# A gated SSM and dense kernel on one core: first tokens turned in 128-row pieces by plain matmuls, first weights on the ScalarE queue, small parameters on the GpSimd queue, B in two parts, third GELU stage ahead of the first outputs

## Chip, cores, metric

The kernel runs on one core of one Trainium2 chip. The metric is the device time of one execution in microseconds (us), as the median of several executions.

Times "at 4.47" are microseconds from the start of the profiled execution's span. The span leaves out about 1.5 to 2 us of the device time, so spans and medians are not mixed in one subtraction.

Names: PE is TensorE, PEld its weight load, DVE is VectorE, ACT is ScalarE, POOL is GpSimd, SP is SyncE. "ACTq" and "SPq" are their instruction streams when they issue DMAs.

## The reference

For 2048 tokens of width 640, the result is `g * a + (1 - g) * b`, where

```python
g = sigmoid((x * gate_w).sum(-1, keepdims=True))
# a: diagonal complex state-space layer (640 states)
dt = exp(log_dt); Lam_bar = exp(dt * Lam)
Bu = einsum("bld,pd->blp", x, ((Lam_bar - 1) / Lam)[:, None] * Bmat)
h[t] = Lam_bar * h[t-1] + Bu[t]
a = 2 * real(einsum("blp,dp->bld", h, Cmat)) + x * Dskip
# b: dense layer, 640 -> 1728 -> 640
b = gelu(x @ w1 + b1) @ w2 + b2
```

Inputs and output are bfloat16.

## The kernel before

The tokens go through in four chunks of 512 (`CH`). For each chunk TensorE does four kinds of stage: the projection by B ("ssm", 50 matmuls of 512 columns), the first dense layer ("FF1"), the second ("FF2", `fin_b`), and the outputs by C (`fin_a`). Chunk 0's FF1 is the first stage, behind a few matmuls without use (the warm-up). For it, half of chunk 0 is transposed on TensorE, from tokens loaded as they lie in memory (`xn`). The other half comes transposed by a DMA. The weights of FF1 are loaded in two blocks: `w1a` (first 6 of 14 column blocks, 192 KB for each of five row blocks) and `w1b`. `prmA` holds three short parameter vectors, 15 rows of 128 numbers; turned into columns on TensorE they feed all of the tables that the scan needs.

The loads, in program order, and the first work:

```python
    load_xn(0, 0, H)                                                    # 320 KB, SP
    nc.scalar.dma_start(out=prmA[0:KS, :], in_=A_log_dt...)             # three small loads, ACT
    nc.scalar.dma_start(out=prmA[KS:2 * KS, :], in_=A_Lambda_im...)
    nc.scalar.dma_start(out=prmA[2 * KS:3 * KS, :], in_=A_Lambda_re...)
    for kd in range(KD):                                                # five times 192 KB, SP
        nc.sync.dma_start(out=w1a[kd][:], in_=B_w1[kd * P:(kd + 1) * P, 0:cut1])
    nc.sync.dma_start_transpose(out=xT[0][:, :, H * P:CH], in_=x2d[H * P:CH, :])
    for kd in range(KD):
        nc.sync.dma_start(out=w1b[kd][:, 0:F - cut1], in_=B_w1[kd * P:(kd + 1) * P, cut1:F])
    make_identity(nc, ident[:])
    # ... (iota and memsets on POOL; prmB on ACT; b1x on SP)
    nc.sync.dma_start_transpose(out=BT_re[:], in_=A_B_re[:, :])
    nc.sync.dma_start_transpose(out=BT_im[:], in_=A_B_im[:, :])
    # ... (further loads)
    for _ in range(6):                                                  # warm-up
        nc.tensor.matmul(wps[:], lhsT=warm[:, 0:P], rhs=warm[:], start=True, stop=True)
    # ...
    for kd in range(KD):
        for a in range(H):
            nc.tensor.transpose(pT[kd][:, a * P:(a + 1) * P], xn[0][:, a, kd * P:(kd + 1) * P], ident[:])
    nc.tensor.transpose(pA[:, 0:3 * KS], prmA[:], ident[0:3 * KS, 0:3 * KS])
    # ... (copies to xT on DVE and ACT; table work)
    for kd in range(KD):                                                # 30 matmuls of 256 columns
        for kf in range(FA):
            ff1_mm(banks[kf], 0, kf, kd, 0, HT)
    # ...
    for kd in range(KD):                                                # 30 more, on the DMA-transposed half
        for kf in range(FA):
            ff1_mm(banks[kf], 0, kf, kd, HT, CH)
```

The order of the stages, as the end of the kernel's text lists them: ssm(0), FF1(1), ssm(1), FF2(0), outputs(0), ssm(2), FF1(2), FF2(1), outputs(1), and so on.

Of the kernel before, what the change touches and what calls it, by code (L numbers as in the profile page):

```python
# [10 lines left out]
ALU = mybir.AluOpType  # L11
ACT = mybir.ActivationFunctionType
BF16 = mybir.dt.bfloat16
F32 = mybir.dt.float32
I32 = mybir.dt.int32
# [12 lines left out]
TPC = CH // P  # L28
HD = D // 2
# [9 lines left out]
def kernel(  # L39
# [32 lines left out]
    def bank(dtype=F32):  # L72
        return ps.tile([P, CH * 4 // (4 if dtype == F32 else 2)], dtype, name="bank")
# [8 lines left out]
    BT_re = const.tile([P, KD, D], BF16, name="BT_re")  # L82
    BT_im = const.tile([P, KD, D], BF16, name="BT_im")
# [5 lines left out]
    prmA = const.tile([3 * KS, P], BF16, name="prmA")  # L89
    NB = KS + KF - 1  # L90
    prmB = const.tile([NB, P], BF16, name="prmB")
# [9 lines left out]
    warm = work.tile([P, CH], BF16, name="v")  # L101
# [8 lines left out]

    H = TPC // 2

    def load_xn(c, a0=0, a1=TPC):
        if a0 == 0:
            xn[c] = xnp.tile([P, TPC, D], BF16, name="xn")
        r0 = c * CH + a0 * P
        nc.sync.dma_start(out=xn[c][:, a0:a1, :], in_=x2d[r0:r0 + (a1 - a0) * P, :].rearrange("(a p) d -> p a d", p=P))

    load_xn(0, 0, H)
    nc.scalar.dma_start(out=prmA[0:KS, :], in_=A_log_dt.rearrange("(j p) -> j p", p=P))  # L120
    nc.scalar.dma_start(out=prmA[KS:2 * KS, :], in_=A_Lambda_im.rearrange("(j p) -> j p", p=P))
    nc.scalar.dma_start(out=prmA[2 * KS:3 * KS, :], in_=A_Lambda_re.rearrange("(j p) -> j p", p=P))
    for kd in range(KD):
        nc.sync.dma_start(out=w1a[kd][:], in_=B_w1[kd * P:(kd + 1) * P, 0:cut1])  # L124
    nc.sync.dma_start_transpose(out=xT[0][:, :, H * P:CH], in_=x2d[H * P:CH, :])  # L125
    for kd in range(KD):
        nc.sync.dma_start(out=w1b[kd][:, 0:F - cut1], in_=B_w1[kd * P:(kd + 1) * P, cut1:F])  # L127
    make_identity(nc, ident[:])
    HC = CH // 4
    tfi = work.tile([P, HC], I32, name="e")  # L130
    nc.gpsimd.iota(tfi[:], pattern=[[1, HC]], base=0, channel_multiplier=0)
    nc.gpsimd.memset(b1x[:, F_LAST:F_LAST + 1], 0.0)
# [3 lines left out]
    nc.scalar.dma_start(out=prmB[KS:NB, :], in_=B_b1[0:(KF - 1) * P].rearrange("(j p) -> j p", p=P))  # L136
    nc.scalar.dma_start(out=prmB[0:KS, :], in_=gate_w.rearrange("(j p) -> j p", p=P))
    nc.sync.dma_start(out=b1x[:, 0:F_LAST], in_=B_b1[F - F_LAST:F].rearrange("(o d) -> o d", o=1).to_broadcast([P, F_LAST]))  # L138
    nc.sync.dma_start_transpose(out=BT_re[:], in_=A_B_re[:, :])  # L139
    nc.sync.dma_start_transpose(out=BT_im[:], in_=A_B_im[:, :])  # L140
# [15 lines left out]
    class Clock:  # L156
        pe = 5.0
        act = 13.0
# [5 lines left out]
    def later(ready, cost, fn):  # L164
        pend.append((ready, cost, fn))

    def let_out(until):
        while pend:
            ready, cost, fn = pend[0]
            start = max(ck.dve, ready)  # L170
            if start >= until:
                return
            pend.pop(0)
            fn()
            ck.dve = start + cost
# [14 lines left out]
    nc.vector.memset(warm[:], 0.0)  # L190
# [3 lines left out]
    wps = bank()  # L194
    for _ in range(6):
        nc.tensor.matmul(wps[:], lhsT=warm[:, 0:P], rhs=warm[:], start=True, stop=True)
    nc.tensor.matmul(wps[:, 0:2 * P], lhsT=warm[:, 0:P], rhs=warm[:, 0:2 * P], start=True, stop=True)
    pA = bank(BF16)
    pT = [bank(BF16) for _ in range(KD)]
    for kd in range(KD):  # L200
        for a in range(H):
            nc.tensor.transpose(pT[kd][:, a * P:(a + 1) * P], xn[0][:, a, kd * P:(kd + 1) * P], ident[:])
    HT = H * P
    nc.tensor.transpose(pA[:, 0:3 * KS], prmA[:], ident[0:3 * KS, 0:3 * KS])

    def col(name, dtype=F32, n=KS):
        return const.tile([P, n], dtype, name=name)
# [7 lines left out]
    for kd in range(KD):  # L215
        dst = xT[0][:, kd, 0:HT]
        if kd % 2 == 0:
            nc.vector.tensor_copy(out=dst, in_=pT[kd][:, 0:HT])
        else:
            nc.scalar.activation(out=dst, in_=pT[kd][:, 0:HT], func=ACT.Identity)  # L220
    nc.vector.tensor_copy(out=colA[:], in_=pA[:, 0:3 * KS])
    nc.scalar.activation(out=dt16[:], in_=ldt_c, func=ACT.Exp)
    nc.vector.tensor_copy(out=dt32[:], in_=dt16[:])
    nc.vector.tensor_tensor(out=dtl[:], in0=dt32[:], in1=lre_c, op=ALU.mult)
    nc.vector.tensor_tensor(out=th_c[:], in0=dt32[:], in1=lim_c, op=ALU.mult)
    nc.vector.tensor_scalar(out=thp_c[:], in0=th_c[:], scalar1=INV_2PI, scalar2=None, op0=ALU.mult)
    nc.scalar.activation(out=r_c[:], in_=dtl[:], func=ACT.Exp)


    scr = gelp.tile([P, KF * CH // 2], F32, name="gel")  # L230
    HB = 2 * HC

    def scratch(i):
        return scr[:, i * KS * HC:(i + 1) * KS * HC].rearrange("p (k i) -> p k i", k=KS)

    u, red, ab = scratch(0), scratch(1), scratch(2)
    m1, m2 = scratch(3), scratch(4)
    FSC = hsp.tile([P, 2 * KS, HB], F32, name="hs")
    FS = FSC[:, 0:KS, :]
    FC = FSC[:, KS:2 * KS, :]  # L240
    NQ = 4
    two = col("two", n=NQ * KS)
    kq = col("kq", I32, n=NQ * KS)
    redq = col("redq", n=NQ * KS)
    absq = col("absq", n=NQ * KS)
    sq = col("sq", n=NQ * KS)
    cq = col("cq", n=NQ * KS)
    kk = work.tile([P, KS, HC], I32, name="bu", bufs=8)

    def over(c):  # L250
        return c.rearrange("p (k o) -> p k o", o=1).to_broadcast([P, KS, HC])

    nc.vector.tensor_tensor(out=u, in0=tf[:].rearrange("p (o i) -> p o i", o=1).to_broadcast([P, KS, HC]), in1=over(thp_c[:]), op=ALU.mult)
    nc.vector.tensor_copy(out=kk[:], in_=u)
    nc.vector.tensor_tensor(out=red, in0=u, in1=kk[:], op=ALU.subtract)
    sth, cth = sq[:, 0:KS], cq[:, 0:KS]
    sL, cL = sq[:, KS:2 * KS], cq[:, KS:2 * KS]
    sH, cH = sq[:, 2 * KS:3 * KS], cq[:, 2 * KS:3 * KS]
    sQ, cQ = sq[:, 3 * KS:4 * KS], cq[:, 3 * KS:4 * KS]


# [3 lines left out]
    def ff1_mm(p, c, kf, kd, t0=0, t1=CH):  # L265
        w = w1a[kd][:, kf * P:(kf + 1) * P] if kf < FA else w1b[kd][:, (kf - FA) * P:(kf - FA + 1) * P]
        nc.tensor.matmul(p[:, t0:t1], lhsT=w, rhs=xT[c][:, kd, t0:t1], start=(kd == 0), stop=(kd == KD - 1))  # L267
        pe(t1 - t0)
# [33 lines left out]
    def ff1(c, k0=0):  # L302
        for kf in range(k0, KF - 1):
            p = bank()
            if kf == KF - 3:
                last = last_bank(c)
            for kd in range(KD):
                ff1_mm(p, c, kf, kd)
            ff1_act(p, c, kf)
            let_out(ck.pe)  # L310
        last_tile(c, *last)
        let_out(ck.pe)

    def gel_tile(c):
        gel[c] = gelp.tile([P, KF, CH], BF16, name="gel")


    gel_tile(0)
    banks = [bank() for _ in range(FA)]
    for kd in range(KD):  # L320
        for kf in range(FA):
            ff1_mm(banks[kf], 0, kf, kd, 0, HT)
# [10 lines left out]
    for kd in range(KD):  # L333
        for kf in range(FA):
            ff1_mm(banks[kf], 0, kf, kd, HT, CH)
        if kd == 2:
            nc.tensor.transpose(pA[:, P:P + NB], prmB[:], ident[0:NB, 0:NB])
            nc.vector.tensor_copy(out=colB[:], in_=pA[:, P:P + NB])
            for j in range(KD):
                nc.vector.tensor_copy(out=w1b[j][:, n1b - 1:n1b], in_=pA[:, P + j:P + j + 1])  # L340
# [69 lines left out]
    def scan_ops(c, ks, bu, ready):  # L410
# [58 lines left out]
        later(0, 0.7, f8)  # L469

    def ssm(c):
        hs[c] = hsp.tile([P, 2 * KS, CH], BF16, name="hs")
        for ks in range(KS):
            bu = work.tile([P, 2, CH], BF16, name="bu", bufs=8)
            for ri, BT in enumerate((BT_re, BT_im)):
                p = bank()
                for kd in range(KD):
                    nc.tensor.matmul(p[:], lhsT=BT[:, kd, ks * P:(ks + 1) * P], rhs=xT[c][:, kd, :],  # L478
                                     start=(kd == 0), stop=(kd == KD - 1))
                    pe(CH)  # L480
                nc.scalar.activation(out=bu[:, ri, :], in_=p[:], func=ACT.Identity)  # L481
                act(0.6)
            scan_ops(c, ks, bu, ck.act)
            if c == 0 and ks == 0:
                later(0, 1.6, factors)
            let_out(ck.pe)
# [27 lines left out]
    def fin_b(c):  # L514
        for a in range(TPC):
# [3 lines left out]
            if a >= TPC - 2:  # L519
                seed(c * TPC + a - (TPC - 2))  # L520
# [12 lines left out]
    def fin_a(c):  # L533
        for a in range(TPC):
# [33 lines left out]
    fin_b(0)  # L568
    fin_a(0)
    load_xn(2)  # L570
    ssm(2)
    gel_tile(2)
    ff1(2)
    fin_b(1)
    gates(2)
# [41 lines left out]
```

## Time and profile before

| | before |
|---|---|
| median of 3 runs (range) | 217.63 us (217.43 to 217.79) |
| span of the profiled execution | 216.2 us |
| PE busy | 211.9 us, 98% |
| first FF1 matmul | 5.26 |
| first projection matmul | 21.13 |
| gapless from, to | 22.49, 213.17 |

The page's first part gives the busy time of each engine, and its second part rows of 40 slices, here the granted TensorE clock in tenths:

```profile
PE 211.9 (98%) x1368; PEld 128.2 (59%) x1368; DVE 189.8 (88%) x393; ACT 91.7 (42%) x156; POOL 1.6 (1%) x12
...
PEclk9999999999999999999999999999999999999999
```

The clock row takes what lies before the first clock change in the trace as full, and that change is the rise at 6.95.

TensorE is the bound. The chain of waits of the kernel before, followed back from the last instruction, shows from where it has been so (columns: start, duration, what; "SPq" is SP issuing a DMA):

```profile
0.73 3.17 DMA xn<-in_A_x_dram
...
4.77 2.04 SPq L125
...
9.85 5.63 SPq L139
...
15.52 6.92 DMA BT_im<-in_A_B_im_dram
...
22.49 9.89 PE bank L478 x45
32.38 14.03 PE bank L267 x65
```

The chain goes through loads until 22.49 and through TensorE alone after that, to 213.17. The timeline of PE in the kernel before shows the first part (columns: start, time, engine, line, operation, names, shapes, count, and in brackets the idle time before and what ended it):

```profile
1.18 2.74 PE L196 MATMUL bank<-v 128*128 128x512 bf16 x6 [1.18 <-DVE halfpi L191]
...
3.95 1.26 PE L202 MATMUL bank<-ident,xn 128*128 128x128 bf16 x10
5.14 0.19 PE L204 MATMUL bank<-ident,prmA 15*128 15x15 bf16 x1
5.26 6.22 PE L267 MATMUL bank<-xT,w1a 128*128 128x256 bf16 x48
...
12.84 5.56 PE L267 MATMUL bank<-xT,w1b 128*128 128x512 bf16 x25
...
21.13 1.24 PE L478 MATMUL bank<-xT,BT_re 128*128 128x512 bf16 x5
22.49 1.25 PE L478 MATMUL bank<-xT,BT_im 128*128 128x512 bf16 x5
```

FF1 starts at 5.26 and goes on with hardly a gap to 21.13; then five projection matmuls, a wait for the imaginary part of B, and no gap any more. If those five matmuls were put in front of 22.49 without the wait, the gapless run would begin at 21.41 (22.49 less 5 x 0.216). The view of one tile gives the time from issue to landing of its loads; this is the line for `w1a`:

```profile
DMA to landing us min/median/max: 3.1/3.5/3.8
```

It covers the landings that the view could assign, here those of the first two of five blocks. The trace keeps every update of the loads' semaphores (counters by which the program waits), and from them the five land at 4.38, 5.59, 6.09, 6.82 and 7.71, at most 3.9 us after their issue.

The view of SP's waits has this line (columns: total us, times, longest):

```profile
SPq L124 <- DMA xn<-in_A_x_dram: 1.3, 1, 1.3
```

The fourth `w1a` (L124) waits until the tokens have landed: 2.65 to 3.92. It is the program that waits. In the trace the loads of SP and ACT take eight semaphores in turn (numbers 100, 102, 103 and 105 to 109), so the ninth load is held until the load that had its semaphore before has landed.

### The profile page before, as it was taken

To read this page: it belongs to the slowest core of one execution; us is meant where nothing else is said; L and a number is where in the kernel's file an instruction comes from. 1 tells how busy PE (TensorE), PEld (TensorE's weight loads), DVE (VectorE), ACT (ScalarE), POOL (GpSimd) and SP (SyncE) were. 2 spreads that over 40 slices of the span, in tenths; PEclk is the share of its full clock that TensorE was granted. 3 is DMA by queue.
4 is the path that set the end of the run, shared out by engine and by line. 5 is a ranking of instruction groups with operands and counts; after the bars stand their busy time and mean duration, and the time that the engine had idled before them with its cause. 6 is when DMAs were issued, how large, how long until landed. Compare 5 with 4: busy or idle time off the path is not lost.

```text
span 216.2 us, 3470 instructions
## 1 busy us (share of the span) xinstructions
PE 211.9 (98%) x1368; PEld 128.2 (59%) x1368; DVE 189.8 (88%) x393; ACT 91.7 (42%) x156; POOL 1.6 (1%) x12
## 2 busy tenths in 40 slices
PE   7999999999999999999999999999999999999994
PEld 3855444454577775444477777444457777777773
DVE  3889999999999899999999999999999999961152
ACT  3689456675696101556642200456662210022100
POOL 2000000000000000000000000000000000000000
PEclk9999999999999999999999999999999999999999
DMA  5999999995000042000010006100001000100011
GB/s 174 255 224 199 226 214 369 175 246 103 3 0 0 0 141 106 0 0 3 0 24 3 0 0 200 45 2 0 0 3 24 0 3 30 61 30 3 2 61 61
DMA packets 32339, 16.16 MB, mean 75 GB/s; under 512 B 25091, under 2 KB 32324, under 8 KB 32324
## 3 DMA queue, kind: packets, MB, share of 16 engines
q1 hardware_dynamic: 32114, 15.91, 30.2%
q8 instruction: 10, 0.16, 0.3%
q10 hardware_dynamic: 210, 0.04, 0.1%
q14 instruction: 5, 0.04, 0.1%
HBM read 7.24 MB, written 2.62 MB: 46 GB/s over the span
## 4 chain that ended last, share of the span: by engine, by line
PE 88%; SPq 5%; DMA 5%; issue 0%; DVE 0%
PE bank L525 28%; PE bank L544 20%; PE bank L478 20%; PE bank L267 19%; DMA BT_im<-in_A_B_im_dram 3%; SPq L139 3%; DMA xn<-in_A_x_dram 1%; SPq L127 1%; SPq L125 1%; PE bank L292 1%; SPq L124 0%; SPq L138 0%; DVE ot L549 0%
## 5 line engine op out<-in xcount | busy, mean ns | idle before, releaser
L525 PE MATMUL bank<-w_sb,gel 128*128 128x320 bf16 x448 | 61.6, 299 | 0.0
L525 PEld LDWEIGHTS <-gel 128*128 128x128 bf16 x448 | 43.6, 98 | 17.2
L481 ACT ACTIVATE bu<-bank 128x512 bf16<-128x512 f32 x40 | 23.9, 597 | 41.7 <-PE bank L478 41.7
L271 ACT ACTIVATE gel<-bank,colB 128x512 bf16<-128x512 f32 x52 | 34.6, 693 | 15.1 <-PE bank L267 14.8
L544 PEld LDWEIGHTS <-hs 128*128 128x128 bf16 x330 | 31.8, 98 | 11.9
L434 DVE TENSOR_TENSOR_SCAN g<-r_c,carry,v 128x512 bf16<-128x512 f32 x30 | 37.2, 1270 | 0.0
L528 ACT ACTIVATE gb<-bank,gcol 128x320 f32<-128x320 f32 x32 | 16.5, 527 | 48.2 <-PE bank L525 46.6
L267 PE MATMUL bank<-xT,w1b 128*128 128x512 bf16 x140 | 31.0, 379 | 0.0
L267 PE MATMUL bank<-xT,w1a 128*128 128x512 bf16 (+1 forms) x150 | 27.6, 344 | 0.0
L544 PE MATMUL bank<-CT_im,hs 128*128 128x320 bf16 (+2 forms) x165 | 27.1, 295 | 0.0
L544 PE MATMUL bank<-CT_re,hs 128*128 128x320 bf16 (+2 forms) x165 | 27.1, 295 | 0.0
L549 DVE SCALAR_TENSOR_TENSOR ot<-bank,gcol,gb 128x320 bf16<-128x320 f32 (+2 forms) x33 | 17.3, 533 | 9.5 <-PE bank L544 9.3
L478 PE MATMUL bank<-xT,BT_im 128*128 128x512 bf16 x100 | 24.9, 379 | 0.1
L478 PE MATMUL bank<-xT,BT_re 128*128 128x512 bf16 x100 | 24.8, 379 | 0.0
L267 PEld LDWEIGHTS <-w1b 128*128 128x128 bf16 x140 | 13.6, 98 | 16.3 <-DMA w1b<-in_B_w_dram 0.3
L267 PEld LDWEIGHTS <-w1a 128*128 128x128 bf16 x150 | 14.9, 100 | 11.7
L511 DVE TENSOR_TENSOR bank<-xn,Dbc 128x320 f32<-128x320 bf16 (+2 forms) x33 | 14.3, 483 | 5.8 <-ACT gb L528 5.8
L478 PEld LDWEIGHTS <-BT_im 128*128 128x128 bf16 x100 | 9.7, 98 | 12.2 <-DMA BT_im<-in_A_B_im_dram 0.6
L478 PEld LDWEIGHTS <-BT_re 128*128 128x128 bf16 x100 | 9.7, 98 | 11.0
L415 DVE TENSOR_TENSOR v<-wa,wb 128x512 bf16<-128x512 bf16 x40 | 15.2, 421 | 0.7
L415 DVE TENSOR_TENSOR wa<-TCOS,g 128x1024 bf16<-128x1024 bf16 x20 | 13.7, 686 | 0.1
L415 DVE TENSOR_TENSOR wb<-TSIN,g 128x1024 bf16<-128x1024 bf16 x20 | 13.7, 684 | 0.0
(98 smaller groups left out, 130.7 us busy)
## 6 DMA issues: line engine op xcount, KB each, us to landing
out_dram<-ot SPq DMA_DIRECT2D x15, 160.0 KB, 1.8
w_sb<-in_B_w_dram SPq DMA_DIRECT2D x1, 2080.0 KB
xn<-in_A_x_dram SPq DMA_DIRECT2D x3, 640.0 KB, 4.9
w1b<-in_B_w_dram SPq DMA_DIRECT2D x5, 240.0 KB, 4.2
w1a<-in_B_w_dram SPq DMA_DIRECT2D x5, 192.0 KB, 3.5
xn<-in_A_x_dram SPq DMA_DIRECT2D x2, 320.0 KB
Dbc<-in_A_Dskip_dram SPq DMA_DIRECT2D x1, 160.0 KB
out_dram<-ot SPq DMA_DIRECT2D x1, 128.0 KB
```

The costliest lines, as they stand in the source:

```text
L139: nc.sync.dma_start_transpose(out=BT_re[:], in_=A_B_re[:, :])
L267: nc.tensor.matmul(p[:, t0:t1], lhsT=w, rhs=xT[c][:, kd, t0:t1], start=(kd == 0), stop=(kd == KD - 1))
L271: nc.scalar.activation(out=gel[c][:, kf, :], in_=p[:, :], func=ACT.Gelu_apprx_tanh, bias=b1_c[:, kf:kf + 1])
L415: nc.vector.tensor_tensor(out=o, in0=a, in1=b, op=op)
L434: nc.vector.tensor_tensor_scan(s["g"][:, ri, :], r_c[:, ks:ks + 1].to_broadcast([P, CH]), s["v"][:, ri, :], init, ALU.mult, ALU.add)
L478: nc.tensor.matmul(p[:], lhsT=BT[:, kd, ks * P:(ks + 1) * P], rhs=xT[c][:, kd, :], start=(kd == 0), stop=(kd == KD - 1))
L481: nc.scalar.activation(out=bu[:, ri, :], in_=p[:], func=ACT.Identity)
L511: dve_now(ck.pe, 0.45, lambda: nc.vector.tensor_tensor(out=p[:, 0:d1 - d0], in0=xn[c][:, a, d0:d1], in1=Dbc[:, d0:d1], op=ALU.mult))
L525: nc.tensor.matmul(p[:, 0:d1 - d0], lhsT=gel[c][:m, kf, lo:lo + P], rhs=w2_sb[:m, kf, d0:d1], start=(kf == 0), stop=(kf == KF - 1))
L528: nc.scalar.activation(out=gb[:, d0:d1], in_=p[:, 0:d1 - d0], func=ACT.Identity, scale=gcol[:, 1, ti:ti + 1])
L544: nc.tensor.matmul(p[:, 0:d1 - d0], lhsT=hs[c][:, j, lo:lo + P], rhs=CT[:, j % KS, d0:d1], start=False, stop=(j == 2 * KS - 1), skip_group ...
L549: nc.vector.scalar_tensor_tensor(out=ot[:, d0:d1], in0=p[:, 0:d1 - d0], scalar=gcol[:, 0, ti:ti + 1], in1=gbs[ti][:, d0:d1], op0=ALU.mult, ...
```

## The change

Its intent is to start FF1 earlier and keep TensorE from waiting in the first 22 us:

- The first tokens come in two loads of 128 rows each, so that FF1 can start on the first 128 columns. They are turned by plain matmuls with the identity instead of transpose mode.
- `w1a` is issued on ACT's queue from the start, in parallel with the tokens on SP. The transposing load of the second half then follows the tokens directly on SP.
- The three `prmA` loads and the small loads behind them move to POOL (`prmA` and `prmB` from ACT, `b1x` from SP).
- B is loaded in two parts, so that the first two of five state blocks come early.
- FF1 of chunk 2 moves ahead of the first outputs, to give DVE more time for its scans.
- The warm-up matmuls read a constant, so that they start before 1.18.

The core of the diff (the FF1 helpers, moved and a little rewritten, the warm-up, the zero-filled tiles of 128 rows for `prmA` and `prmB`, and the bookkeeping of the static schedule are cut):

```diff
-    load_xn(0, 0, H)
-    nc.scalar.dma_start(out=prmA[0:KS, :], ...)            # and two more
+    load_xn(0, 0, 1)
+    load_xn(0, 1, H)
     for kd in range(KD):
-        nc.sync.dma_start(out=w1a[kd][:], in_=B_w1[kd * P:(kd + 1) * P, 0:cut1])
-    nc.sync.dma_start_transpose(out=xT[0][:, :, H * P:CH], in_=x2d[H * P:CH, :])
+        nc.scalar.dma_start(out=w1a[kd][:], in_=B_w1[kd * P:(kd + 1) * P, 0:cut1])
+    nc.sync.dma_start_transpose(out=xT[0][:, :, HT:CH], in_=x2d[HT:CH, :])
+    make_identity(nc, ident[:])
+    nc.gpsimd.memset(prmA[:], 0.0)
+    nc.gpsimd.dma_start(out=prmA[0:KS, :], ...)            # and two more
     for kd in range(KD):
         nc.sync.dma_start(out=w1b[kd][:, 0:F - cut1], ...)
-    make_identity(nc, ident[:])
 ...
-    nc.scalar.dma_start(out=prmB[KS:NB, :], ...)           # prmB (2)
-    nc.sync.dma_start(out=b1x[:, 0:F_LAST], ...)
+    nc.gpsimd.dma_start(out=prmB[KS:NB, :], ...)           # prmB (2), b1x, behind the iota
 ...
-    nc.sync.dma_start_transpose(out=BT_re[:], in_=A_B_re[:, :])
-    nc.sync.dma_start_transpose(out=BT_im[:], in_=A_B_im[:, :])
+    for r0, r1, part in ((0, KSA * P, 0), (KSA * P, KS * P, 1)):
+        nc.sync.dma_start_transpose(out=BT_re[part][:], in_=A_B_re[r0:r1, :])
+        nc.sync.dma_start_transpose(out=BT_im[part][:], in_=A_B_im[r0:r1, :])
 ...
-            nc.tensor.transpose(pT[kd][...], xn[0][:, a, kd * P:(kd + 1) * P], ident[:])
+        nc.tensor.matmul(p[:, col:col + P], lhsT=xn[0][:, a, kd * P:(kd + 1) * P], rhs=ident[:], ...)
 ...
+    strip(0, 0, P, True)                                   # 6 matmuls of 128 columns
+    ...                                                    # the second 128 rows are turned
+    strip(1, 0, P, False)
+    nc.tensor.matmul(pA[:, P:P + 3 * KS], lhsT=prmA[:], rhs=ident[:, 0:3 * KS], ...)
+    ...
+    strip(0, P, HT, False)
+    strip(1, P, HT, False)
+    for kd in range(2, KD):
+        strip(kd, 0, HT, False)
 ...
     fin_b(0)
+    gel_tile(2)
+    ff1(2, 0, (0, 1))
+    gates(2)
     fin_a(0)
     load_xn(2)
     ssm(2)
-    gel_tile(2)
-    ff1(2)
```

## The prediction

> **What bounds the kernel now.** TensorE. The page shows PE busy for 211.9 of 216.2 us (98%), DVE 189.8 (88%), ACT 91.7. The chain of waits is gapless matmuls from 22.49 to 213.17 us: 10.79 us for 50 projection matmuls (0.216 us each), 14.64 for an FF1 stage, 15.24 for an FF2 stage, 10.87 for an output stage. So those 190.7 us can't shrink by reordering; only the first 22.5 us and the 3 us after the last matmul (untouched by the change) can.
>
> **The start, before** (timeline). Warm-up matmuls from 1.18; first tokens (320 KB) land at 3.90; transposes to 5.2; FF1 from 5.26 to 21.13; five projection matmuls; then PE waits for B_im, which lands at 22.45 (0.3 us lost). The SP queue carries the chain there: w1a issues to 4.7, a transpose 2.04, w1b, b1x, B_re 5.63, B_im 6.92 to landing. Counting starts per quarter us, PE runs 256-column matmuls at about 3 per 0.25 us until 7.0 and 4 to 5 after: about 0.9 us is lost to the cold clock after 5.26. Other waits for w1a and w1b: 0.2 + 0.2 + 0.3.
>
> **The change.**
> - First tokens in two 160 KB DMAs; w1a issued on the ACT queue from 0.73 instead of 1.25: first piece and weights land at my estimate 3.3. FF1 starts with 128-column strips at about 4.2 instead of 5.26. Worth 1 us.
> - Plain matmuls for transposes: [...] Here the clock rose only at about 7.0 although PE was busy from 1.18; no run yet shows the cause.[...]
> - 24 strips of 128 columns:[...] costs at most 0.5 us.
> - B in two parts: the first lands an estimated 4 us sooner (of 1.6 MB at 160 to 290 GB/s); the second is needed 4.3 us later. B wait gone (0.3). w1b issues 2 to 3 us earlier: 0.3 to 0.5 gone.
> - Small parameters move to the POOL queue, iota behind three of them. DVE's index conversion waits for iota and stands ahead of the first copies; PE's parameter matmul also waits. May cost 0.5 us or more.
> - FF1(2) before the first outputs moves 14.6 us of PE work, removes none. By my sum (6.5 us per scan group) DVE's first output seeds come at 82 to 84.5 us; PE needs them at about 86. Before, they were ready 1 to 3 us ahead, and a faster start would have eaten most of that. It keeps slack, gains nothing itself.
>
> **Sum.** 1.0[...] + 0.3 + 0.5 - 0.4 (narrow strips) - 0.3 (POOL risk) = 1.6 us, all in the first 22.5 us. Predicted 216.0 us, eight in ten between 215.0 and 217.0. Faster by over 2%: 0.03; within 2%: 0.95; slower: 0.02.
>
> **What would show it.** First FF1 matmul near 4.2; first projection matmul near 19.8 with no wait for B; 256-column matmuls at full rate before 7; then an unbroken chain of matmuls of about 191.8 us; no PE wait on DVE at the first outputs; DVE busy about unchanged.
>
> **What would make it wrong.** POOL's DMAs delaying iota or parameters by over 1 us; w1a starved by the transpose sharing the DMA engines; DVE tables finishing later so that seeds come after 86 us and PE waits; clock rising late again.

The sum came to 1.6 us. Its term "+ 0.5 (clock)" and the ground for it in the second bullet are cut, because no trace or run shows that ground; the terms left come to 1.1 us, while the 216.0 us stand on the full sum. For the price of the strips, the 0.4 us stand as estimate alone. At the full clock the matmuls of the first strip of the kernel after start 55 ns apart (from 4.47 to 4.74), and their weight loads of 95 to 98 ns overlap. The rates "3" and "4 to 5" fit the trace of the kernel before if matmuls and weight loads are counted together. The matmuls alone are the 11 in 1.75 us and the 41 in 4.45 us; at the later pace the 11 take 1.19 us, so by my estimate 0.56 us were lost before 6.95, not 0.9.

## More of the kernel before

From 5.20 to 6.95 the trace has 11 matmuls in 1.75 us of busy time, and from 6.95 to 11.40 it has 41 in 4.45 us.

## The result, and the profile after

| | before | after |
|---|---|---|
| median (range), 4 runs each | 217.71 us (217.43 to 218.07) | 223.51 us (222.60 to 223.83) |
| ratio, 95% interval | | 1.0259 (1.0233 to 1.0286) |
| span of the profiled execution | 216.2 us | 221.6 us |
| first FF1 matmul | 5.26 | 4.47 |
| first projection matmul of the gapless run | 21.41 (worked out above) | 26.47 |
| end of the last matmul | 213.17 | 218.22 |
| from that to the end | 191.76 | 191.75 |

A ratio here is the mean time of one kernel's fast runs over that of the other kernel's fast runs of the same rounds, so it is not quite the ratio of the medians that stand beside it.

The change makes the kernel slower by 2.6%. The lower rows say where. The gapless run is as long as before to 0.01 us, and FF1 begins 0.79 us sooner, as wanted, but the gapless run begins 5.06 us later. The loss lies between 4.47 and 26.47.

The same lines of the page for the kernel after:

```profile
PE 212.4 (96%) x1370; PEld 129.4 (58%) x1381; DVE 189.3 (85%) x393; ACT 91.4 (41%) x156; POOL 5.2 (2%) x20
...
PEclk9669999999999999999999999999999999999999
```

PE is busy about as long and DVE is unchanged. The clock row now has two slices (5.5 to 16.6 us) at six tenths. The timeline of PE in the kernel after shows the hole:

```profile
3.80 0.67 PE L202 MATMUL bank<-ident,xn 128*128 128x128 bf16 x5
4.47 0.49 PE L237 MATMUL bank<-xT,w1a 128*128 128x128 bf16 x6
5.18 0.45 PE L202 MATMUL bank<-ident,xn 128*128 128x128 bf16 x5 [0.21 <-DMA xn<-in_A_x_dram]
5.47 0.50 PE L237 MATMUL bank<-xT,w1a 128*128 128x128 bf16 x6
10.12 0.17 PE L308 MATMUL bank<-ident,prmA 128*128 128x15 bf16 x1 [4.15 <-DMA prmA<-in_A_Lambda_re_dram]
10.14 6.88 PE L237 MATMUL bank<-xT,w1a 128*128 128x128 bf16 x48
...
18.19 5.56 PE L237 MATMUL bank<-xT,w1b 128*128 128x512 bf16 x24
...
26.47 1.24 PE L508 MATMUL bank<-xT,BT_re 128*128 128x512 bf16 x4
```

TensorE does its two narrow strips, then stands 4.15 us before a matmul of 15 columns, because the third of the small parameter loads has not landed. There is no wait for B any more. The chain of waits of the kernel after names the same load, issued by POOL at 2.62 and taking 7.36 us for 1.2 KB:

```profile
2.12 0.51 POOL prmA L126
2.62 7.36 DMA prmA<-in_A_Lambda_re_dram
...
10.29 6.73 PE bank L237 x48
```

The views of the tiles give the landing times; in the kernel after, first `prmA`:

```profile
DMA to landing us min/median/max: 4.5/7.0/7.4
```

and then `w1a`:

```profile
DMA to landing us min/median/max: 2.8/4.5/7.1
```

So the bulk weights are late as well. This line lacks the fourth block; from the semaphore updates the five land at 3.57, 4.94, 6.93, 9.55 and 10.69. The fourth takes 7.4 us and the fifth 7.1, against at most 3.9 before. The transposing load is issued 3.08 us sooner than before (at 4.77, above), as SP's timeline in the kernel after shows:

```profile
1.69 1.96 SPq L122 DMA_TRANSPOSE xT<-in_A_x_dram  x1
```

Before the fifth `w1b` SP then waits for that load to land (10.22), as the view of its waits says:

```profile
SPq L129 <- DMA xT<-in_A_x_dram: 4.2, 1, 4.2
```

What was issued between 1.69 and 6 us, on any queue, landed between 9.1 and 13.2.

Views by stretches of time complete the picture. First the stretch from 5 to 9 us, before (columns: stretch, its length, PE busy with the number of matmuls, granted clock, share of the DMA engines' time, GB/s):

```profile
5.00:9.00 4.00, 4.00 (x30) 1.00 1.00 225
```

The same and three more of the kernel after:

```profile
5.00:9.00 4.00, 0.79 (x11) 0.84 1.22 144
...
4.29:7.71 3.41, 1.45 (x20) 1.00 1.10 168
10.20:14.50 4.30, 4.30 (x28) 0.50 1.12 347
15.00:16.80 1.80, 1.80 (x19) 1.00 0.95 187
```

After the change the DMA engines are fully booked from 5 to 9 us (1.22; the share is over 1, so packets' times overlap) but move only 144 GB/s, while the transposing load is in flight (1.69 to 10.22). The view of the DMA queues of the kernel after for this stretch says whose time it is (columns: packets, MB, share of the 16 engines):

```profile
q1 hardware_dynamic: 1187, 0.30, 72.0%
q10 hardware_dynamic: 201, 0.28, 47.8%
q0 software_dynamic: 64, 0.00, 2.1%
```

q1 is SP's queue, with the transposing load in it, q10 ACT's with the weights, and q0 POOL's. Two streams are served side by side, booked on the same 16 engines: q1 moved 0.30 MB in 1187 packets (250 bytes each on average), q10 0.28 MB in 201 (1.4 KB each). Before, q1 alone had 1712 packets and 0.90 MB in the same stretch, 100.1%.

And the clock is half from 7.71 to 14.54: 28 matmuls in 4.30 us, where 19 took 1.80 us once it was full again (the stretches mix widths of 128 and 256 columns).

The 5.06 us add up as follows. The earlier first FF1 matmul gives 0.79, and the B wait that is gone gives 0.28 (21.41 less 21.13). Waits cost 4.15 + 0.21. The rest, 1.77 (5.06 + 0.79 + 0.28 - 4.36), is the difference in what the FF1 work itself took. The half clock and the price of the pieces are in it; the experiments ask how much of it is clock.

### The profile page after: what moved, and what is told of

It reads as the page before. It is cut to its first block, busy times and chain, and to the rows that moved or that the text cites. A ratio compares the mean times of both kernels' runs of the same rounds, so it can differ in the third digit from the quotient of the medians.

```text
span 221.6 us, 3494 instructions
## 1 busy us (share of the span) xinstructions
PE 212.4 (96%) x1370; PEld 129.4 (58%) x1381; DVE 189.3 (85%) x393; ACT 91.4 (41%) x156; POOL 5.2 (2%) x20
## 3 DMA queue, kind: packets, MB, share of 16 engines
HBM read 7.24 MB, written 2.62 MB: 44 GB/s over the span
## 4 chain that ended last, share of the span: by engine, by line
PE 94%; DMA 3%; POOL 1%; issue 0%; DVE 0%; POOLq 0%
PE bank L555 28%; PE bank L237 26%; PE bank L575 20%; PE bank L508 19%; DMA prmA<-in_A_Lambda_re_dram 3%; PE bank L263 1%; POOL prmA L125 0%; POOL prmA L126 0%; DVE ot L580 0%; POOL ident masks.py:199 0%; POOL prmA L124 0%; PE bank L308 0%; PE bank L253 0%; POOL ident masks.py:197 0%; POOLq L632 0%
## 5 line engine op out<-in xcount | busy, mean ns | idle before, releaser
L237 PE MATMUL bank<-xT,w1a 128*128 128x512 bf16 (+2 forms) x159 | 29.0, 343 | 0.2
L237 PEld LDWEIGHTS <-w1a 128*128 128x128 bf16 x162 | 16.2, 107 | 11.9
L445 DVE TENSOR_TENSOR wb<-TSIN,bu 128x1024 bf16<-128x1024 bf16 x20 | 13.7, 687 | 0.0
```

The costliest lines, as they stand in the source:

```text
L237: nc.tensor.matmul(p[:, t0:t1], lhsT=w, rhs=xT[c][:, kd, t0:t1], start=(kd == 0) if first is None else first, stop=(kd == KD - 1), skip_gr ...
L445: nc.vector.tensor_tensor(out=o, in0=a, in1=b, op=op)
```

## The experiments

Every experiment kernel but one computes the right result. The letters in the quoted expectations: A, the small parameter loads are slow because POOL issues them; B, the weights on ACT come late, because the transposing load now stands beside them; C, a further cost in the other small loads or in the pieces; D, the loads of the start crowd one another, whoever issues them.

### 1. Undoing parts of the change, cumulatively: `a1_prmA_act`, `a2_w1a_sp`, `a3_small_act`

`a1_prmA_act` (after, with the `prmA` rows on ACT behind the first of `w1a`, in a 15-row tile):

```diff
+    nc.scalar.dma_start(out=w1a[0][:], ...)
-    nc.gpsimd.dma_start(out=prmA[...], ...)     # three
+    nc.scalar.dma_start(out=prmA[...], ...)     # three
+    for kd in range(1, KD): nc.scalar.dma_start(out=w1a[kd][:], ...)
```

> The changed kernel with one part undone: the three rows of SSM parameters (1.2 KB each) go on the ACT queue right behind the first weight tile, instead of on POOL; all else as changed. Theory A (the late landing of these parameters at 9.98 us is the whole loss: 4.15 us of TensorE waiting, and about 2.2 us at half clock after it): the time falls by over 5.5 us to 216.0 to 217.0 us, first projection matmul near 20 us. Rival B (a second, hidden cost: w1a tiles 3 and 4 and the transposed half of x land only at 9.55, 10.69 and 10.22 us because the transpose on the SP queue shares the DMA engines with the weights on the ACT queue; before, w1a was in by about 8.1): TensorE now waits for weights between 7 and 10.7 us, the first projection matmul comes near 22 us, time 218 to 219 us. The parameters land by 6 us in both.

Measured: 221.62 us (221.31 to 221.89), ratio 1.0183 (1.0167 to 1.0200). The wait for `prmA` is gone, and PE waits 1.94 us for the second of `w1a` instead (landed at 7.76); the clock drops at 7.04 and comes back at 13.87, and the first projection matmul is at 25.41. The loss has moved from one load to the next. The time lies above both expectations. The run is not clean: the parameter rows push the second of `w1a` to an issue at 2.41.

`a2_w1a_sp` (a1, and `w1a` back on SP between tokens and transposing load, so `prmA` is first on ACT):

```diff
-        nc.scalar.dma_start(out=w1a[kd][:], ...)
+        nc.sync.dma_start(out=w1a[kd][:], ...)
```

> As a1, and the five w1a tiles back on the SP queue between the tokens and the transpose, as before; the ACT queue carries only the three parameter rows. Theory A: no better than a1, if anything 0.3 us worse because the first weights are issued later. Rival B: w1a lands by about 8 us, the waits for it go, and the time falls by 1 to 2 us against a1. In both: the biases on the POOL queue (landing at 12 us in the changed kernel) are needed by TensorE at about 11 us and may now show a wait of up to 1 us.

Measured: 218.66 us (218.30 to 218.77), ratio 1.0050 (1.0033 to 1.0066). First projection matmul at 21.21, and the clock never falls after 4.96. That is 3.0 us under a1, more than B gave.

`a3_small_act` (a2, and `prmB` and `b1x` on ACT too):

```diff
-    nc.gpsimd.dma_start(out=prmB[...], ...); nc.gpsimd.dma_start(out=b1x[...], ...)
+    nc.scalar.dma_start(out=prmB[...], ...); nc.scalar.dma_start(out=b1x[...], ...)
```

> As a2, and the remaining small loads (biases, gate weights, last bias row) also moved from POOL to the ACT queue. Rival B with a third cost C (biases on POOL land at about 12 us, needed at about 11): 0.3 to 1 us faster than a2, and between 215.5 and 217 us, that is 0.5 to 2 us under the kernel before. If the biases on POOL cost nothing: equal to a2 within 0.3 us.

Measured: 218.38 us (217.90 to 218.68), ratio 1.0033 (1.0016 to 1.0050). The difference to a2 is within both intervals. The 215.5 to 217 us of cost C were missed: a third cost in these small loads is not seen (0.3 us at most); a rest of 0.3 to 0.5% over the kernel before stays in both.

### 2. POOL alone, on the kernel before: `a4_before_prmA_pool`

The kernel before, with only the three `prmA` loads on POOL, and one more such load in mid-kernel, when the queues are quiet:

```diff
-    nc.scalar.dma_start(out=prmA[...], ...)     # three
+    nc.gpsimd.dma_start(out=prmA[...], ...)     # three, behind make_identity
 ...
+    nc.gpsimd.dma_start(out=prmA[0:KS, :], in_=A_log_dt...)   # probe, ahead of the folding of C
```

> The kernel before, with only the three parameter rows moved from the ACT to the POOL queue (and, as a probe, one of them loaded once more on POOL near 57 us, when the DMA engines are idle). Theory A and B: TensorE waits for the parameters from 5.1 us until they land; landing at 7 to 10 us gives 2 to 5 us of waiting[...]: 219.5 to 224 us. The probe tells why the landing is late: if the cost is the traffic of the other queues, the same 1.2 KB lands within 2 to 3 us when the engines are idle; if the POOL path is slow by itself, it takes 4.5 to 7.4 us there as well.

Measured: 218.96 us (218.77 to 220.46), ratio 1.0077 (1.0042 to 1.0112); the prediction of this run was too high. The view of `prmA`'s tile, where the smallest value is the quiet probe:

```profile
  DMA prmA<-in_A_Lambda_re_dram: 1.6, 1
...
DMA to landing us min/median/max: 2.9/3.4/3.5
```

A POOL load of 1.2 KB takes 2.9 us from the start of its issue with nothing else moving (0.52 us of it the issue), and 3.3 to 3.5 us in the start of the kernel before. PE waits 1.6 us for it there, and the clock doesn't drop. So POOL explains less than half of a landing time of 7.4 us, and of a wait of 4.15.

### 3. Undoing one line only: `b1_only_w1a_sp`

The kernel after, with `w1a` issued on SP again between the tokens and the transposing load. `prmA` stays on POOL:

```diff
-        nc.scalar.dma_start(out=w1a[kd][:], in_=B_w1[kd * P:(kd + 1) * P, 0:cut1])
+        nc.sync.dma_start(out=w1a[kd][:], in_=B_w1[kd * P:(kd + 1) * P, 0:cut1])
```

> The changed kernel with only w1a put back on the SP queue, between the tokens and the transpose of x; the SSM parameters stay on POOL. Theory D (the root is that the ACT queue's weights and the SP queue's transpose run at once and hold up everything, the POOL loads too): the parameters land by about 6.5 us instead of 9.98 (in the kernel before with the parameters on POOL they landed at 6.20), TensorE waits under 1 us for them, the clock doesn't drop, first projection matmul at 21 to 22 us, time 218 to 219.5 us. Rival A (POOL by itself is what is late): landing stays at 9 us or more, TensorE waits 3 us or more, time 221 us or more.

Measured: 218.59 us (218.12 to 219.44), ratio 1.0038 (1.0007 to 1.0070). One line of issue order gives back 4.9 of the 5.8 us. The timeline of PE in this run:

```profile
5.07 0.82 PE L237 MATMUL bank<-xT,w1a 128*128 128x128 bf16 x6 [0.82 <-DMA w1a<-in_B_w_dram]
...
7.41 0.17 PE L308 MATMUL bank<-ident,prmA 128*128 128x15 bf16 x1 [0.35 <-ACT xT L211]
7.43 5.26 PE L237 MATMUL bank<-xT,w1a 128*128 128x128 bf16 x48
...
22.15 1.24 PE L508 MATMUL bank<-xT,BT_re 128*128 128x512 bf16 x5
```

and the line of `prmA`'s tile for it:

```profile
DMA to landing us min/median/max: 3.1/3.4/3.8
```

The three `prmA` loads are issued at the same times as in the kernel after (1.5 to 2.6), by the same engine, and now land in 3.1 to 3.8 us; nobody waits for them. What changed is what else was in flight: SP issues one `w1a` block each 0.47 us, and the transposing load only at 4.03 (after: 1.69). Theory A, that POOL by itself makes these loads late, is refuted for the kernel after. Theory D gave all of this but the first projection matmul, which is just later than its 21 to 22 in this execution, the slowest of the four (219.44), where the clock rose only at 8.52 (after: 4.30). Which of the loads in flight does the crowding, this run can't tell; part 5 asks it.

### 4. The parameters off the critical path: `b2_param_late`

The kernel after; no DMA is moved. The parameter matmul and all that hangs on it go behind the first-half strips in program order:

```diff
-    nc.tensor.matmul(pA[:, P:P + 3 * KS], lhsT=prmA[:], ...)   # and the column work
     strip(0, P, HT, False)
     strip(1, P, HT, False)
     for kd in range(2, KD):
         strip(kd, 0, HT, False)
+    nc.tensor.matmul(pA[:, P:P + 3 * KS], lhsT=prmA[:], ...)   # and the column work
```

> The changed kernel with only TensorE's parameter matmul (and the DVE and ACT work that hangs on it) put behind the strips of the first half, so that TensorE doesn't stand still for the parameters; no DMA is moved. Theory A (the wait for the parameters is the whole loss): TensorE runs on through 6 to 10 us, first projection matmul near 21 us, 217 to 218.5 us. Theory D: it now waits for w1a tiles 3 and 4 and for x, which land at 9.55 to 10.7 us, the clock still drops, and only 1 to 3 us come back: 220.5 to 222.5 us.

Measured: 224.03 us (222.97 to 225.05), ratio 1.0283 (1.0237 to 1.0330): no gain at all, more than expected. The timeline of PE in this run:

```profile
10.25 2.00 PE L237 MATMUL bank<-xT,w1a 128*128 128x256 bf16 x12 [2.96 <-DMA w1a<-in_B_w_dram]
...
18.00 4.27 PE L237 MATMUL bank<-xT,w1b 128*128 128x512 bf16 x19 [1.07 <-DVE w1b L370]
```

With `prmA` out of the way, PE waits for the fourth block of `w1a` until nearly the same time (10.25), the clock drops later (at 11.06), and DVE's work, which starts late, adds a wait of 1.07. The wait that the profile of the kernel after names is only one of two that end close together. Taking `prmA` off the path gains nothing here, in part because DVE's late work has its own price; a1, which repaired its landing, gained 1.9 us.

### 5. What crowds: `b3_transpose_late` and `h1_plain_half`

`b3_transpose_late` (after, the transposing load of x behind `w1b` on SP):

```diff
-    nc.sync.dma_start_transpose(out=xT[0][:, :, HT:CH], ...)
     ...
     for kd in range(KD):
         nc.sync.dma_start(out=w1b[kd][:, 0:F - cut1], ...)
+    nc.sync.dma_start_transpose(out=xT[0][:, :, HT:CH], ...)
```

> The changed kernel with only the order on the SP queue altered: the transpose of the second half of the first tokens is issued behind the five w1b loads instead of ahead of them; w1a stays on ACT and the parameters on POOL. If it is the transpose's many small packets that hold up the other queues: parameters land by 7 us and w1a by 9 us, and the time falls to 219 to 221.5 us, though the second half of x then lands late, at 11 to 13 us. If any bulk load on the SP queue does the same: parameters at 9 us or later, no better than 223 us.

Measured: 220.72 us (220.41 to 221.34), ratio 1.0135 (1.0112 to 1.0158). `prmA` lands 5.0 to 5.3 us after issue, PE waits 2.14, the first projection matmul is at 23.84. Half of the loss comes back, as expected, though `prmA` (7.92) and `w1a` (9.63) land later than the 7 and 9 that went with it.

`h1_plain_half` (after, but the same bytes loaded in the same place by a DMA that does not transpose; its result is wrong, relative error 0.032):

```diff
-    nc.sync.dma_start_transpose(out=xT[0][:, :, HT:CH], in_=x2d[HT:CH, :])
+    nc.sync.dma_start(out=xT[0][:, :, HT:CH], in_=x2d[HT:CH, :].rearrange(...))
```

> The changed kernel with the second half of the first tokens loaded by a plain DMA of the same bytes instead of a transposing one; the result is wrong on purpose (its time is what counts), nothing else is moved. If the transpose, not the number of bytes, is what holds up the ACT queue's weights and the POOL queue's parameters: parameters land by 7.5 us, the last w1a tile by 9 us, TensorE waits under 2 us at the parameter matmul, time under 220 us. If any load of that size beside them does it: parameters at 9 us or later, 222 us or more.

Measured: 220.38 us (218.79 to 220.80), ratio 1.0091 (1.0058 to 1.0124), between the two expectations. `prmA` lands 3.4 to 5.6 us after issue, PE waits 2.38, and the first projection matmul is at 23.90. In the stretch from 5 to 9 us (columns as above) this run shows:

```profile
5.00:9.00 4.00, 1.62 (x24) 0.89 1.01 344
```

The kernel after had 144 GB/s there, with the engines no less busy (1.22). So a stretch with the transposing load in flight beside other loads can book the DMA engines without moving much. It need not: with that load in flight too, the kernel before moved 225 GB/s there, `b1_only_w1a_sp` 256 and `a4_before_prmA_pool` 286, but `d3_small_pool`, with all weights on SP, only 169. The place and kind of the transposing load account for about half of the loss, the clock's share included (in both runs the half clock lasts 3.41 us instead of 6.83). The other half stays when the load is plain, and also when it is moved away altogether (b3): in both runs `w1b` is then issued early on SP (from 1.66 in b3, 2.40 in h1), most of `prmA` still takes over 5 us, and PE still waits over 2 us.

### 6. The move alone, on the kernel before: `f1_before_w1a_act`

The kernel before, with nothing changed but `w1a` on ACT, behind the parameter rows:

```diff
-        nc.sync.dma_start(out=w1a[kd][:], ...)
+        nc.scalar.dma_start(out=w1a[kd][:], ...)
```

> The kernel before with only the five w1a loads moved from the SP to the ACT queue, behind the three parameter rows: is the move that the changed kernel can't stand enough to break the kernel before? Theory D (weights on ACT and the transpose on SP run at once and delay each other): w1a's last tiles land at 9.5 to 11 us instead of about 8, TensorE waits for them among the first strips, its clock drops or rises late, first projection matmul at 23 to 26 us, time 219.5 to 223 us. Rival (only the parameters' way over POOL matters): within 0.5 us of the kernel before.

Measured: 224.33 us (223.16 to 224.90), ratio 1.0281 (1.0249 to 1.0312). It is enough by itself for the whole loss, which is more than I expected, and it shows a second way to lose. The first projection matmul is at 28.14, later than either expectation. The timeline of ACT in this run:

```profile
1.96 4.72 ACTq L124 DMA_DIRECT2D w1a<-in_B_w_dram  x5
7.82 0.33 ACTq L136 DMA_DIRECT2D prmB<-in_B_b_dram  x1
...
9.27 1.28 ACT L220 ACT_TABLE_LOAD   x1 [9.27 <-DMA w1a<-in_B_w_dram]
10.56 0.66 ACT L220 ACTIVATE xT<-bank 128x256 bf16<-128x256 bf16 x2
```

ACT's DMA issues come first in its stream, and the later of them are spread out to 8.95: the issues take 3.8 us in all, and in the rest of the time ACT waits for semaphores of earlier loads (that of `prmB` at 7.82 for the second `w1a`, the next for a `w1b` of SP). Its first computation, the copy of transposed tokens that PE needs, comes after them. In the kernel before that copy starts at 4.60, behind a table load at 2.66; here at 10.56, behind one at 9.27. PE waits 0.83 for `prmA` (though ACT issues it), 0.65 for `w1a`, and 2.46 for this copy, and the clock rises only at 16.47. So the sum is as large as in the kernel after, though the path is not the same: the kernel after has its table load on ACT at 3.99, behind issues that end at 3.96. The crowding is there as well: by the semaphore updates the last two of `w1a` land at 10.06 and 10.66, so TensorE would have had to wait for them if ACT had not been held.

### 7. The clock's share: `g1_filler`

The kernel after, with 20 useless matmuls of 384 columns ahead of the parameter matmul, to keep TensorE busy through the wait:

```diff
+    for _ in range(20):
+        nc.tensor.matmul(pA[:, P:512], lhsT=ones(P), rhs=ones(384), start=True, stop=True, ...)
     nc.tensor.matmul(pA[:, P:P + 3 * KS], lhsT=prmA[:], ...)
```

> The changed kernel with 20 matmuls of 384 columns of ones put ahead of the parameter matmul (their result is overwritten, the output stays right): TensorE is busy for about 3.3 of the 4.15 us in which it waits, no wait is removed. If the drop of the clock costs what I read (6.8 us at half clock, of which 4.35 us with work: about 2.2 us): the clock stays up, the matmuls after 10.1 us run at full rate, first projection matmul at 24.3 us, time 221 to 221.7 us. If w1a's and x's late landing (10.2 to 10.7 us) binds there instead: less than 1 us comes back, 222.5 us or more.

Measured: 222.15 us (221.18 to 222.46, 5 runs), ratio 1.0195 (1.0170 to 1.0221). The view by stretches in this run:

```profile
10.00:14.50 4.50, 4.50 (x49) 1.00 1.29 285
```

The clock stays up, and 49 matmuls fit where 28 did. The profiled execution, which was this kernel's fastest, has its first projection matmul at 24.27, 2.2 us sooner than the kernel after; the medians differ by 1.4 us. The wait for `prmA` stays as it was (the matmul is at 10.04). So 1.4 to 2.2 us of the loss is the half clock that the wait brings after it, and it is extra to the wait. The median missed the expected 221 to 221.7, and the comparison is not quite clean: in the profiled execution the clock rose at 6.05, against 4.30 in the kernel after.

### 8. The other parts of the change: `c1_before_order`, `e1_split_order`, `d2_best_try`, `d3_small_pool`

`c1_before_order` (before, with FF1 of chunk 2 and its seeds moved as in the change):

```diff
     fin_b(0)
+    gel_tile(2)
+    ff1(2, 0, (0, 1))
+    gates(2)
     fin_a(0)
```

> The kernel before with only the third GELU stage (and the seeds and the emission rule that go with it) moved ahead of the first outputs. My prediction: it moves TensorE's work and removes none, 217.4 to 217.9 us, ratio within 0.3% of 1. Rival: it delays DVE work or holds PSUM banks, and TensorE waits at the first outputs: 218.5 us or more.

Measured: 217.98 us (217.86 to 218.04), ratio 1.0004 (0.9986 to 1.0023). Neutral by the ratio, as predicted; the median is 0.08 us above the range given.

`e1_split_order` (c1, and B in two parts; 5 rounds):

```diff
+    for r0, r1, part in ((0, KSA * P, 0), (KSA * P, KS * P, 1)):
+        nc.sync.dma_start_transpose(out=BT_re[part][:], ...)
+        nc.sync.dma_start_transpose(out=BT_im[part][:], ...)
```

> The kernel before with only two parts of the change: B in two parts and the third GELU stage ahead of the first outputs. My prediction: the wait for B goes (0.3 us), nothing else moves: 217.2 to 217.6 us. It also tells what the pieces of the first tokens cost: the run with all small loads on ACT and w1a on SP has these two parts and the pieces as well and was 0.7 us slower than the kernel before.

Measured: 217.70 us (217.34 to 218.04), ratio 0.9983 (0.9965 to 1.0002). The wait for B is gone and the first projection matmul is at 20.81. This is the good part of the change, but it is worth 0.2%, and the interval includes no gain.

`d2_best_try` (e1, with the two token loads, the warm-up from a constant and `b1x` on ACT):

```diff
-    load_xn(0, 0, H)
+    load_xn(0, 0, 1)
+    load_xn(0, 1, H)
```

> A version built to beat both: as the run before this one, and the first tokens in two loads (but one transpose step), warm-up matmuls from the constant (TensorE starts at 0.78 instead of 1.18 us), the last bias row on ACT instead of SP; all weights stay on SP. FF1 starts at about 4.7 instead of 5.26 us: 216.4 to 217.2 us. If the first weight tile, now issued 0.4 us later, is what FF1 waits for: no gain over the run before.

Measured: 218.13 us (217.97 to 218.34), ratio 1.0003 (0.9986 to 1.0020). No gain: a second token load puts the first of `w1a` at 1.66 instead of 1.25 on the same queue. FF1 starts at 4.82, later than the 4.72 of e1.

`d3_small_pool` (e1, with `prmB` and `b1x` on POOL; 5 rounds):

```diff
-    nc.scalar.dma_start(out=prmB[...], ...); nc.sync.dma_start(out=b1x[...], ...)
+    nc.gpsimd.dma_start(out=prmB[...], ...); nc.gpsimd.dma_start(out=b1x[...], ...)
```

> A second attempt at a version that beats both: the kernel before with B in two parts and the third GELU stage moved (217.70 us, ratio 0.998 to the kernel before), and the biases, gate weights and last bias row on POOL behind iota; the SSM parameters stay on ACT and all weights on SP. With three fewer loads[...] the last w1a tiles and the transpose are issued about 1 us sooner. If the pace of the weights' landing bounds the start: 216.7 to 217.3 us. If not: 217.5 to 218 us, and the loads on POOL (needed at 11 us) land by 8 us in both.

Measured: 219.35 us (219.01 to 219.42), ratio 1.0063 (1.0051 to 1.0076): a miss. It was meant to let the transposing load be issued earlier, and it did (3.79, against 4.70 in e1). But the third and fourth of `w1a` then land at 8.21 and 8.66, and PE waits 1.59 for them. This is the same direction as in the kernel after. Why a4, with the transposing load at about the same time, showed no such wait for `w1a` is left open.

No kernel tried beats the kernel before clearly.

## Why the prediction was wrong

Predicted were 216.0 us, between 215.0 and 217.0, with a chance of 0.02 for slower. Measured were 223.51 us. The direction was wrong, and by much more than the range.

**The step that failed** is the first bullet of the change: "w1a issued on the ACT queue from 0.73 instead of 1.25: first piece and weights land at my estimate 3.3. FF1 starts with 128-column strips at about 4.2 instead of 5.26. Worth 1 us." It costed the time of the issue and took the time to landing as fixed. The first weights did come early (3.57), FF1 did start early (4.47), and 0.79 of its 1 us came. But the move to a second queue also took away what had spaced the loads: SP's own pace of one issue in 0.47 us, and in the kernel before its wait from 2.65 to 3.92 for the tokens to land. With `w1a` gone from SP, the transposing load was issued at 1.69 instead of 4.77 and `w1b` from 3.70 instead of 6.86. The work then stood beside the loads that TensorE needed next: the last two of `w1a` took 7.4 and 7.1 us instead of at most 3.9, and `prmA` 7.4. One line undone returns 4.9 of 5.8 us (`b1_only_w1a_sp`), and the one line alone in the kernel before costs 2.8%, in part by another path (`f1_before_w1a_act`).

What the step missed is in the trace of the kernel after: from 5 to 9 us SP's queue had 72.0% of the 16 engines' time, ACT's 47.8% and POOL's 2.1%, and the loads issued on ACT, POOL and SP between 1.69 and 6 us all landed at 9.1 or later. Why order on one queue protected `w1a` in b1 (landings at most 4.2 us after issue where the view assigns them), and a second queue didn't, is not shown by any run. Order on one queue can't be the whole account: in `d3_small_pool` the third and fourth of `w1a` were issued on SP 1.57 and 1.10 us ahead of the transposing load and still took 6.0 us each. That the transposing load comes earlier, and not that the weights have a second queue, may be the larger part; no run has the one without the other and the rest unchanged. The prediction named the sharing only among the risks.

**The mis-sized term** is "- 0.3 (POOL risk)", and, under the change, "May cost 0.5 us or more". It measured 4.15 us of wait, plus the clock. POOL's own part is smaller: in the kernel before, POOL loads took 3.3 to 3.5 us and cost 1.6 us of wait (`a4_before_prmA_pool`). With the kernel after's own program and `w1a` on SP, nobody waits for them (`b1_only_w1a_sp`). The rest is crowding.

**Steps that the list of risks named, but to which the odds gave nothing:** "POOL's DMAs delaying iota or parameters by over 1 us", "w1a starved by the transpose sharing the DMA engines", and "clock rising late again". The parameters, the weights and the clock all did so, the clock by dropping. They are not independent: one cause, the early transposing load and the rest beside it, brought the first two, and the waits brought the third (a1 and b2 lose the clock by a wait for `w1a`, and g1, kept busy, keeps it). Odds of 0.02 treated them as unlikely one by one. The second was hidden in the profile of the kernel after, behind the first; `a1_prmA_act` and `b2_param_late` brought it out.

**The clock.** The prediction gave up to 0.5 us of gain from the clock, for plain matmuls in place of transpose mode. That was the author's estimate; no run isolated it. The clock did rise earlier in the kernel after (4.30, against 6.95 before), but `e1_split_order`, which keeps transpose mode, had it at 3.96 and `c1_before_order` at 6.46; of the runs with plain matmuls, `a1_prmA_act` had it at 3.63 and `b1_only_w1a_sp` at 8.52. So the spread from run to run is as large as the supposed effect. What counted was the drop after the wait: 1.4 to 2.2 us (`g1_filler`). In the kernel after the clock rose at 4.295, fell at 7.708 and rose again at 14.535, that is 3.413 us later and twice that. TensorE did not stand still for all of the time before a fall: in the 3.41 us before it PE was busy 0.81 (`b2_param_late`), 1.03 (`h1_plain_half`), 1.18 (`b3_transpose_late`), 1.45 (after) and 1.48 us (`a1_prmA_act`). In `a4_before_prmA_pool` it was busy 1.81 of the 3.41 us from 4.09 on, and no fall came. The length of these windows is taken from the spacing in the kernel after.

**What was right.** TensorE bounds the kernel, and the rest of it is a fixed 191.75 us. The B wait is gone. The moved FF1 stage is neutral (`c1_before_order`), and TensorE waits for no seed at the first outputs: the last seeds are done at 90.7, and the first output matmul is at 92.58. DVE's busy time is unchanged. The iota made DVE's index conversion wait until 3.44, as feared, but DVE's first copy of turned tokens was due at 4.12 anyway. The price of narrow strips and pieces was put at 0.4 us. It was not measured alone; a3, which has all of the change but the moved loads, stands at 1.0033, and e1, without the pieces, at 0.9983. By that the early start by pieces is no gain but costs about 0.5%, on the order of 1 us. The two were not timed in the same rounds, and a3 also has its token loads in two, which `d2_best_try` makes responsible for a part of it.

**What stays open.** About half of the loss goes with the transposing load (`b3_transpose_late`, `h1_plain_half`). How the rest divides between `w1b`, `w1a` and the POOL loads was not taken apart, nor was what in the DMA engines delays the small loads. The transposing load was not measured alone. Why `d3_small_pool` suffers with a transposing load at 3.79 and `a4_before_prmA_pool`, with one at 3.72, does not is not known either.

## What to carry to other kernels

Before moving a load to an idle issuing queue, ask what the old queue was holding back: the load that follows it there will be issued sooner (here the transposing load at 1.69 instead of 4.77), and will be in flight beside everything that is urgent. Put small loads on which a chain depends ahead of the bulk, and cost a load by its time from issue to landing with the traffic it will meet, not by its issue (here 1.2 KB on POOL took 2.9 us alone and up to 7.4 us in the start of the kernel after). A wait that the profile names can hide a second one that ends at the same time (here at 10.12 and, in `b2_param_late`, 10.25), so undo the cause and not the wait; and count the clock that a long wait of TensorE can lose after it (here 1.4 to 2.2 us after a wait of 4.15).
